# A six-layer cross network on one core: the order of the last but one group's output transposes, and of the first products and sums of the last layer

## The chip, the core and the metric

The kernel runs on one NeuronCore of a Trainium2 chip. It has a matrix engine (PE, with its weight loads shown as PEld), a vector engine (DVE), a scalar engine (ACT), GpSimd (POOL) and a queue engine (SP), which here issues nearly all DMA transfers. Each engine executes its own instructions in order and waits on semaphores for the others. The metric is the device time of one execution in microseconds (us); lower is better. What is compared is the median of several executions.

## The reference

```python
B, F, D, L = 16384, 26, 16, 6          # x0: 16384 x 416, ws: 6 x 416 x 416, bs: 6 x 416, all bfloat16
x = x0
for l in range(L):
    proj = jnp.einsum('bd,de->be', x, ws[l]) + bs[l]
    x = x0 * proj + x
return x
```

Each of the six layers is a 416 x 416 product over 16384 rows, a bias, an elementwise product with `x0` and an elementwise sum with the layer's input.

## The kernel before

The 16384 rows are cut into 8 groups of 2048 (`g` = 0 to 7). Inside the core the data lie transposed: features on the partitions, rows along the free axis. The 416 features are three tiles of 128 (`t` or `i` = 0, 1, 2) and a tail of 32 (`x3`); the four chunks of 512 rows of a group (`j` = 0 to 3) have their tails stacked in one 128-partition tile. A pair (group, layer) is a job; a list written out by hand interleaves the jobs of several groups so that PE always has one that is ready.

A tile of a job is computed by `full` (12 matmuls of 128x128 by 512, line L456) and `rows32` (the tail's 4 matmuls, L477), and read out of PSUM by `evacuate`: ACT adds the bias (L394), DVE multiplies by `x0` (L403) and adds the layer's input (L408). The tails of several jobs are computed together (`tails`, L471, L488, L497; read out by L434, L436, L438).

The program is recorded by `Program.add`: the place where an instruction is recorded is its place in its engine's queue, and its waits follow from the tiles that it reads and writes. Nothing reorders it later, save that DVE's sums in `evacuate` are held back by one product.

**Groups 0 to 6** leave the chip through `output(g)`. The result lies transposed, so SP issues DMA transposes into the tile `ost`: `turn(0)`, `turn(1)` and `turn(2)` (L637), one for each feature tile of 128 x 2048, and one for the tail tile into `ot3` (L643). The tail is then spread over `ost` by a copy (`spread`: POOL for groups 0 to 5, ACT for group 6, L663), and `store` (L672) writes `ost` to HBM. For group 6, the last but one (`g == LAST - 1`), the third tile's transpose comes in two halves, and the spread and the two stores of half a group each are recorded by the caller, after all tiles of layer 4 of group 7. Each of group 6's transposes has a semaphore (lane) of its own.

**Group 7** takes another way in its last layer, so that its result needs no transpose: `nat_full` multiplies with the data as the stationary operand (L797, with the tail and bias matmuls of `nat_rows` at L840 and L845), so rows lie on the partitions. ACT copies each 128 x 416 result out of PSUM (`nat_out`, L851), DVE multiplies two of them by `x0` (`nat_mul`, L857), adds the layer's input (`nat_add`, L863), and `nat_store` (L870) writes four of them out. There are 16 such results: four steps `kk` of four chunks `j`. In step 0 DVE does, for each pair of chunks, the product and then the sum.

The layer's input that `nat_add` needs, `x5n`, must be turned as well, from layer 4's result. Its first two feature tiles are turned by DMA: `rest_turn(0)` and `rest_turn(1)` (L683), issued by SP. Its third tile and its tail are turned on PE (`turn_last`, L808; `turn_tails`, L826) and copied by DVE (L820) and ACT (L818, L833). Every `nat_add` waits for both DMA transposes.

At the end of the program SP's queue holds, in this order:

```
rest_turn(0)      L683   needs tile (7, layer 4, i=0)
turn(0)           L637   needs tile (6, layer 5, i=0)
tail transpose    L643   needs the tail of (6, layer 5)
turn(1)           L637   needs tile (6, layer 5, i=1)
turn(2) in halves L637   needs tile (6, layer 5, i=2)
rest_turn(1)      L683   needs tile (7, layer 4, i=1)
two stores        L672   group 6
four stores       L870   group 7 (a fifth is issued by ACT)
```

The tiles are computed in the order (6, layer 5, i=0), (6, layer 5, i=1), the tails, (6, layer 5, i=2), (7, layer 4, i=1), (7, layer 4, i=2).

Of the kernel before, what the change touches and what calls it, by code (L numbers as in the profile page):

```python
# [21 lines left out]
class Program:  # L22
# [12 lines left out]
    def add(self, eng, fn, reads=(), writes=(), lane=None, batch=None, hold=False, release=False):  # L35
        op = Op(eng, fn, lane, batch)
        deps = {}
        if eng == "pool":
            writes = list(writes) + ["pool"]
        for t in reads:  # L40
            w = self.writer.get(t)
            if w is not None:
                deps[id(w)] = (w, True)
        for t in writes:
            w = self.writer.get(t)
            if w is not None:
                deps[id(w)] = (w, True)
            for r in self.readers.get(t, ()):
                if id(r) not in deps:
                    deps[id(r)] = (r, False)  # L50
        for d, raw in deps.values():
            if d.lane is None and d.eng == eng and lane is None and (eng == "pe" or not raw):
                continue
            op.deps.append(d)
        for t in reads:
            self.readers.setdefault(t, []).append(op)
        for t in writes:
            self.writer[t] = op
            self.readers[t] = []
        if eng == "dve":  # L60
            if hold:
                self.flush()
                self.held = op
            else:
                self.queue[eng].append(op)
                if release:
                    self.flush()
        else:
            self.queue[eng].append(op)
        if lane is not None:  # L70
            batches = self.lanes.setdefault(lane, [])
            if not batches or batches[-1][0] != batch:
                batches.append((batch, []))
            batches[-1][1].append(op)
        return op
# [123 lines left out]
def bass_standalone__cross_network_dcn__recsys_kernel(  # L199
# [14 lines left out]
    LAST = NG - 1  # L214
# [136 lines left out]
    def done_with(g, l):  # L351
        users[(g, l)] = users.get((g, l), 0) + 1
        if users[(g, l)] < 2:
            return
        if l > 0:
            free_x.append(xset[(g, l)])
            free_3.append(xtail[(g, l)])
        prefill(g, l + 1)
        if l == L - 1:
            output(g)  # L360
            if g == 3:
                load_last()
            if 4 < g + NX0 <= LAST:
                load_group(g + NX0)
# [268 lines left out]
    def output(g):  # L633

        s, s3 = xset[(g, L)], xtail[(g, L)]
        def turn(t, j0=0, j1=NJ):
            add("sp", lambda h: h.dma_start_transpose(  # L637
                ost[:, j0 * KK:j1 * KK, t * P:(t + 1) * P], xs[s][:, t * GC + j0 * CH:t * GC + j1 * CH]),
                reads=[("x", s, t, j) for j in range(j0, j1)], writes=[("ost", t, j) for j in range(j0, j1)],
                lane="ot" if g < LAST - 1 else f"ot_{t}{j0}", batch=g)  # L640

        turn(0)
        add("sp", lambda h: h.dma_start_transpose(ot3[:, :, :], x3s[s3][:, :]),  # L643
            reads=[("x3", s3)], writes=["ot3"], lane="ot3", batch=g)
        if g < LAST - 1:
            spread("pool")
        turn(1)
        if g < LAST - 1:
            turn(2)
            store(g, 0, NJ)  # L650
        else:
            turn(2, 0, 2)
            turn(2, 2, NJ)
        free_x.append(s)
        free_3.append(s3)

    def spread(eng):

        dst = ost[:, :, NT * P:D].rearrange("p (j k) f -> p j k f", j=NJ)
        sp_ = ot3[:, :, :].rearrange("p k (j f) -> p j k f", j=NJ)  # L660
        kw = dict(reads=["ot3"], writes=[("ost", NT, j) for j in range(NJ)])
        if eng == "act":
            add("act", lambda h: h.activation(dst, sp_, ACT_F.Copy), **kw)  # L663
        else:
            add(eng, lambda h: h.tensor_copy(dst, sp_), **kw)  # L665

    def store(g, j0, j1):

        rows = out[g * GC + j0 * CH:g * GC + j1 * CH, :]
        o = ost[:, j0 * KK:j1 * KK, :].rearrange("p (j k) f -> p j k f", k=KK)  # L670
        pat = "(j p k) f -> p j k f" if g == 0 else "(j k p) f -> p j k f"
        add("sp", lambda h: h.dma_start(rows.rearrange(pat, j=j1 - j0, k=KK), o),  # L672
            reads=[("ost", t, j) for t in range(NT + 1) for j in range(j0, j1)],
            writes=[("out", g, j0)], lane="out", batch=g)
# [108 lines left out]
    g, l = LAST, L - 1  # L783
# [70 lines left out]
    def nat_mul(kk, j, n=2):  # L854
        o, x0v = on[:, j:j + n, kk, :], x0n7[:, j:j + n, kk, :]
        toks = [("on", a, kk) for a in range(j, j + n)]
        add("dve", lambda h: h.tensor_tensor(o, o, x0v, ALU.mult),  # L857
            reads=toks + [("n7", a) for a in range(j, j + n)], writes=toks)

    def nat_add(kk, j, n=2):  # L860
        o, x5v = on[:, j:j + n, kk, :], x5n[:, j:j + n, kk, :]
        toks = [("on", a, kk) for a in range(j, j + n)]
        add("dve", lambda h: h.tensor_tensor(o, o, x5v, ALU.add),  # L863
            reads=toks + [("x5n", a, t) for a in range(j, j + n) for t in range(NT + 1)], writes=toks)
# [3 lines left out]
    def nat_store(kk, j0, j1, eng="sp"):  # L868
        dst = out[LAST * GC:B, :].rearrange("(j k p) f -> p j k f", j=NJ, k=KK)[:, j0:j1, kk, :]
        add(eng, lambda h: h.dma_start(dst, on[:, j0:j1, kk, :]),  # L870
            reads=[("on", j, kk) for j in range(j0, j1)],
            writes=[("out7", kk, j0)], lane=f"out7_{stores[0]}", batch=0)
        stores[0] += 1
# [18 lines left out]
    turned_out(2, b2)  # L892
    for j in (0, 2):
        nat_mul(0, j)
        nat_add(0, j)
    nat_store(0, 0, NJ)
    nat_rows(1, bks[1])
# [54 lines left out]
```

## Time and profile before

| what | value |
|---|---|
| median of 4 runs | 479.81 us (478.33 to 480.57) |
| the profiled execution | 479.09 us, span 477.3 us |
| granted PE clock | 0.997 |
| PE busy | 468.2 us (98% of the span) |
| DVE busy | 403.7 us (85%) |
| ACT busy | 342.0 us (72%) |
| POOL busy | 6.6 us (1%) |
| PE's share of the chain that ended last | 90% |

The span runs from the first to the last instruction of the profiled execution; its 479.09 us hold 1.8 us more than that. Times below are counted from the span's start. PE is busy almost all the time until 471 us; what follows is the end of group 7: DVE's products and sums, and the stores. Short forms in the views: "SPq" and "ACTq" are the queues in which these engines issue transfers; "idle before <-releaser" gives the time that an engine stood idle before an instruction and what it was waiting for.

### The profile page before, as it was taken

The numbers are of one execution on the slowest core, as the hardware profiler recorded it, in microseconds if no ns is written. First come the engines' busy times: TensorE is split into PE (matmuls) and PEld (weight loads), VectorE is DVE, ScalarE is ACT, GpSimd is POOL, SyncE is SP. The second block draws the span as 40 slices with busy tenths as digits, with TensorE's granted clock in tenths as the row PEclk, the third lists the DMA queues.
The fourth block names the chain that finished last, engine by engine and source line by source line (L and its number), as shares of the span: only waits on it lengthen the run. The fifth ranks groups of instructions, "written<-read, shape, count | busy, mean of one in ns | idle before, by whom it ended". The sixth has DMA issues, their size and how long they took to land.

```text
span 477.3 us, 8393 instructions
## 1 busy us (share of the span) xinstructions
PE 468.2 (98%) x3371; PEld 195.9 (41%) x3371; DVE 403.7 (85%) x696; ACT 342.0 (72%) x372; POOL 6.6 (1%) x15
## 2 busy tenths in 40 slices
PE   7999999999999999999999999999999999999994
PEld 6344444444444444444444444444444444444342
DVE  2888888888888888898889879888888888888877
ACT  3677777777777777777777777777777777777684
POOL 1000000000000000000000000000000000000000
PEclk9999999999999999999999999999999999999998
DMA  8976940630102377379319931980000138026899
GB/s 228 175 161 134 207 86 1 145 77 1 28 7 45 66 215 161 78 151 239 75 26 206 211 89 31 188 246 0 2 15 20 21 64 236 2 45 151 204 143 287
DMA packets 138363, 53.31 MB, mean 112 GB/s; under 512 B 112330, under 2 KB 137428, under 8 KB 138324
## 3 DMA queue, kind: packets, MB, share of 16 engines
q1 hardware_dynamic: 137448, 52.14, 48.8%
q10 hardware_dynamic: 876, 0.64, 0.4%
q8 instruction: 26, 0.43, 0.4%
q14 instruction: 13, 0.11, 0.1%
HBM read 5.97 MB, written 13.63 MB: 41 GB/s over the span
## 4 chain that ended last, share of the span: by engine, by line
PE 90%; SPq 4%; DVE 3%; DMA 2%; ACT 0%; issue 0%; DVEq 0%
PE ps L456 75%; PE ps L477 7%; PE ps L497 7%; SPq L292 2%; DMA x<-x 1%; PE ps L471 1%; DVE x L863 1%; DVE x L857 1%; PE ps L488 1%; SPq L297 1%; DVE tw L403 1%; DVE x L408 1%; SPq L285 1%; SPq L521 0%; ACT tw L394 0%; DMA x<-ost 0%
## 5 line engine op out<-in xcount | busy, mean ns | idle before, releaser
L394 ACT ACTIVATE tw<-ps,bias 128x1024 bf16<-128x1024 f32 (+1 forms) x295 | 299.5, 1070 | 120.2 <-PE ps L477 76.0
L456 PE MATMUL ps<-x,wm 128*128 128x512 bf16 x1692 | 379.4, 380 | 0.4 <-DMA wm<-in_ws_dram 0.4
L456 PEld LDWEIGHTS ps<-x,wm 128*128 128x128 bf16 x1692 | 158.9, 98 | 214.0 <-issue 28.5
L403 DVE TENSOR_TENSOR tw<-tw,x 128x1024 bf16<-128x1024 bf16 (+1 forms) x285 | 192.7, 685 | 53.8 <-ACT tw L394 53.5
L408 DVE TENSOR_TENSOR x<-tw,x 128x1024 bf16<-128x1024 bf16 (+1 forms) x285 | 182.1, 679 | 0.0
L477 PE MATMUL ps<-x,w 32*128 32x512 bf16 x512 | 39.3, 379 | 0.1
L497 PE MATMUL ps<-x,wm 128*32 128x512 bf16 x564 | 33.0, 380 | 0.0
L434 ACT ACTIVATE ts<-ps,bias 128x512 bf16<-128x512 f32 x47 | 28.7, 700 | 0.0
L438 DVE TENSOR_TENSOR x<-ts,x 128x512 bf16<-128x512 bf16 x47 | 18.6, 417 | 3.1 <-DMA x<-x 3.0
L497 PEld LDWEIGHTS ps<-x,wm 128*32 128x32 bf16 x564 | 13.8, 96 | 17.6 <-issue 5.3
L477 PEld LDWEIGHTS ps<-x,w 32*128 32x128 bf16 x512 | 7.8, 92 | 27.7 <-issue 27.1
L436 DVE TENSOR_TENSOR ts<-ts,x 128x512 bf16<-128x512 bf16 x47 | 18.5, 417 | 0.0
L665 POOL COPY ost<-ot 128x512 bf16<-128x512 bf16 x6 | 5.2, 864 | 423.5 <-DMA ot<-x 423.5
L797 PE MATMUL ps<-wm,x 128*128 128x416 bf16 x48 | 9.5, 340 | 0.0
L568 DVE COPY x<-ps 128x512 bf16<-128x512 bf16 x4 | 1.7, 424 | 8.9 <-PE ps L561 8.9
L851 ACT ACTIVATE x<-ps 128x416 bf16<-128x416 f32 x16 | 7.7, 534 | 2.0 <-PE ps L797 1.9
L565 ACT ACTIVATE x<-ps 128x512 bf16<-128x512 bf16 x8 | 4.2, 599 | 5.8 <-PE ps L561 5.8
L863 DVE TENSOR_TENSOR x<-x,x 128x832 bf16<-128x832 bf16 x8 | 4.7, 592 | 2.6 <-DMA x<-x 2.3
L797 PEld LDWEIGHTS ps<-wm,x 128*128 128x128 bf16 x48 | 4.3, 98 | 4.2 <-issue 1.0
L488 PE MATMUL ps<-x,w 32*32 32x512 bf16 x188 | 5.9, 374 | 0.0
L471 PE MATMUL ps<-x,w 32*32 32x512 bf16 x208 | 5.6, 385 | 0.0
L561 PE MATMUL ps<-ident,x 128*128 128x128 bf16 x64 | 5.3, 243 | 0.3 <-ACT x L565 0.3
(38 smaller groups left out, 35.8 us busy)
## 6 DMA issues: line engine op xcount, KB each, us to landing
out_dram<-ost SPq DMA_DIRECT2D x6, 1664.0 KB, 7.0
x<-in_x_dram SPq DMA_DIRECT2D x7, 416.0 KB, 8.0
x<-x SPq DMA_DIRECT2D x24, 96.0 KB, 2.2
out_dram<-ost SPq DMA_DIRECT2D x2, 832.0 KB, 6.6
wm<-in_ws_dram SPq DMA_DIRECT2D x5, 312.0 KB, 3.5
x<-x SPq DMA_DIRECT2D x22, 64.0 KB, 2.0
out_dram<-x SPq DMA_DIRECT2D x3, 416.0 KB, 3.8
x<-ost SPq DMA_DIRECT2D x28, 32.0 KB, 2.3
```

The source lines that it names most:

```text
L394: add("act", lambda h, a=a, w=w, b0=b0: h.activation(tw[r][:, a * CH:(a + w) * CH], psum[:, b0 * CH:(b0 + w) * CH], ACT_F.Identity, bias=b ...
L403: add("dve", lambda h, a=a, e=e: h.tensor_tensor(tw[r][:, a * CH:e * CH], tw[r][:, a * CH:e * CH], x0s[s0][:, i * GC + a * CH:i * GC + e * ...
L408: add("dve", lambda h, a=a, e=e: h.tensor_tensor(xs[so][:, i * GC + a * CH:i * GC + e * CH], tw[r][:, a * CH:e * CH], src(i, a, e), ALU.ad ...
L434: add("act", lambda h: h.activation(ts[r][:, :], bank(b), ACT_F.Identity, bias=bias[:, 3, l:l + 1], scale=1.0), reads=[("ps", b), "bias"], ...
L436: add("dve", lambda h: h.tensor_tensor(ts[r][:, :], ts[r][:, :], x03, ALU.mult), reads=[("ts", r)] + tok0, writes=[("ts", r)], release=True)
L438: add("dve", lambda h: h.tensor_tensor(x3s[so][:, :], ts[r][:, :], res, ALU.add), reads=[("ts", r)] + rtok, writes=[("x3", so), ("x3", so, ...
L456: add("pe", lambda h, t=t, j=j: h.matmul(bank(banks[j]), wm[l][:, t, ecols], src(t, j, j + 1), start=(first and t == 0), stop=(not first a ...
L471: add("pe", lambda h, q=q, j=j, r=r, c=c, o=o: h.matmul(psum[o, banks[j] * CH:(banks[j] + 1) * CH], w3[l][q, i * P + c * T32:i * P + (c + ...
L477: add("pe", lambda h, q=q, j=j, r=r: h.matmul(bank(banks[j]), w3[l][q, ecols], src[q, :], start=first, stop=not first, tile_position=(r * ...
L488: add("pe", lambda h, l=l, b=b, s3=s3, ri=ri, qi=qi, ro=ro, qo=qo: h.matmul(psum[qo, b * CH:(b + 1) * CH], w3[l][qi, NT * P:D], s3[qi, :], ...
L497: add("pe", lambda h, t=t, j=j, src=src, l=l, b=b, ro=ro, qo=qo: h.matmul(psum[qo, b * CH:(b + 1) * CH], wm[l][:, t, NT * P:D], src(t, j, ...
L797: add("pe", lambda h, t=t: h.matmul(bank(b, n=D), xcol(t, j, kk), wm[l][:, t, :], start=(first and t == 0), stop=(not first and t == NT - 1)),
```

## The change

In `output`, for group 6 alone, `turn(1)` is recorded right after `turn(0)`, ahead of the tail's transpose. For the other groups the order stays. In the last layer of group 7, step 0 (four chunks, two to an instruction) does both products before the first sum; in steps 1 to 3 the order stays.

```diff
         turn(0)
+        if g == LAST - 1:
+            turn(1)
         add("sp", lambda h: h.dma_start_transpose(ot3[:, :, :], x3s[s3][:, :]),
             reads=[("x3", s3)], writes=["ot3"], lane="ot3", batch=g)
         if g < LAST - 1:
             spread("pool")
-        turn(1)
-        if g < LAST - 1:
+            turn(1)
             turn(2)
             store(g, 0, NJ)
         else:
@@
     turned_out(2, b2)
     for j in (0, 2):
         nat_mul(0, j)
+    for j in (0, 2):
         nat_add(0, j)
     nat_store(0, 0, NJ)
```

The numbers of instructions on each engine stay the same. Lines from L643 on move by one or two numbers in the changed file (L643 becomes L645, L683 L684, L857 L858, L863 L864).

## The prediction

> **What bounds the kernel now.** The page's list of the chain that ended last comes first: PE has 90% of it, but a change at the very end lives in the other tenth. So I read the chain in order of time over the last 80 us. PE's matmuls run through until 453 us; then the chain leaves PE:
>
> ```profile
> 459.51 0.67 DVE tw L403 x2
> 460.18 0.14 DVE x L408
> 460.32 5.56 DMA x<-x
> 465.88 0.03 issue
> ...
> 466.00 0.59 DVE x L863
> 466.59 0.51 DVE x L857
> ...
> 467.20 0.59 DVE x L863
> ```
>
> The 5.56 us are one transfer, `rest_turn(1)`, from its issue to its landing; DVE's first sum (L863) starts on it, and from there sum and product alternate to the last sum. The timeline of DVE's and ACT's instructions tells how hard that hold is:
>
> ```profile
> 458.22 1.28 DVE L408 TENSOR_TENSOR x<-tw,x 128x1024 bf16<-128x1024 bf16 x2
> 463.09 0.59 DVE L857 TENSOR_TENSOR x<-x,x 128x832 bf16<-128x832 bf16 x1 [0.30 <-ACT x L851]
> 466.00 0.59 DVE L863 TENSOR_TENSOR x<-x,x 128x832 bf16<-128x832 bf16 x1 [2.31 <-DMA x<-x]
> 459.74 0.67 ACT L663 ACTIVATE ost<-ot 128x512 bf16<-128x512 bf16 x1
> 462.13 1.75 ACT L851 ACTIVATE x<-ps 128x416 bf16<-128x416 f32 x4 [0.89 <-PE ps L797]
> 469.56 2.10 ACT L851 ACTIVATE x<-ps 128x416 bf16<-128x416 f32 x4 [0.58 <-PE ps L797]
> ```
>
> DVE sits idle for 2.31 us between its first product and its first sum. ACT has copied out all four results of step 0 by 462.13 + 1.75 = 463.88, and all of step 3 by 471.66, while DVE's last sum starts at 474.10: after the first sum DVE alone sets the pace, with some 2 us of lead on ACT. Third, SP's queue, which issued the transfer:
>
> ```profile
> 449.15 2.94 SPq L637 DMA_TRANSPOSE ost<-x  x1
> 453.92 1.19 SPq L643 DMA_TRANSPOSE ot<-x  x1
> 455.15 5.13 SPq L637 DMA_TRANSPOSE ost<-x  x3
> 460.32 1.94 SPq L683 DMA_TRANSPOSE x<-x  x1
> 462.44 3.23 SPq L672 DMA_DIRECT2D out_dram<-ost  x2
> ```
>
> SP stood still from 452.09 (449.15 + 2.94) to 453.92, waiting for the tail, and then issued without a break. The tile that `rest_turn(1)` turns was ready at 459.50 (458.22 + 1.28), yet it went out at 460.32: 0.8 us behind the queue. Last, the DMA in short stretches (length, granted clock, DMA share, GB/s):
>
> ```profile
> 453.00:455.00 2.00, 1.00 0.02 5
> 456.40:458.70 2.30, 1.00 1.09 209
> 461.50:462.80 1.30, 1.00 1.67 210
> 462.80:464.40 1.60, 1.00 0.94 10
> 464.40:465.30 0.90, 1.00 1.21 273
> ```
>
> From 453 to 455 nothing moved. A whole tile of 524 KB takes some 2.4 us at 209 GB/s. And in the middle of `rest_turn(1)` the transfers all but halt for 1.6 us, from 462.8 to 464.4.
>
> **The change part by part.** No instruction is added or taken away; two are moved.
>
> *`turn(1)` ahead of the tail's transpose (SP).* Its tile is ready when the second L408 of that tile ends, at 452.55 by DVE's timeline; SP is free at 452.09. So it goes out at 452.6. A full transpose that SP issues with nothing behind it has taken 1.39 (455.15) to 1.98 us (446.70), so it is out by 454.0 to 454.6. It holds up one thing, the tail's transpose, ready at 453.88: out 0.1 to 0.7 us later than before, ending at 455.2 to 455.8 with its 1.19 us, or 456.6 with the longest of that line (2.04 us, at 249.97, behind a full one). For whom is that late? The two halves of `turn(2)` wait for DVE's sums at 456.43 and 457.03 anyway, so for them nothing is; and ACT's spread (L663) reads the tail. That copy comes only after ACT's other work, at 459.74. The tail landed 2.4 us after its issue here and 3.5 at most elsewhere, so by 454.6 + 3.5 = 458.1 in the changed order. It costs nothing; without that cover every us after 459.74 would delay ACT by one.
>
> The first half goes out at 456.5, where it went before (456.58): its data hold it. But the halves took 2.02 and 1.62 us to issue because a full tile was still under way ahead of them. With the DMA nearly drained I put a half between the quarter (1.19 us) and the full tile (1.98): 1.45 us each. 456.5 + 2 x 1.45 = 459.4, just ahead of `rest_turn(1)`'s data at 459.50. So `rest_turn(1)` goes out at 459.55, 0.77 us earlier. The bounds: 0.1 us if the halves take their old 2.02 + 1.62 us (456.5 + 3.64 = 460.2), and 0.8 us at best, by the data.
>
> *What the landing makes of it.* In the profile the first packets came 1.2 us after the issue (460.32 to 461.5). From 459.55 they start at 460.7. By 462.8 they have run 2.1 us x 209 GB/s = 439 of 524 KB. If the halt stays where it is, the remaining 85 KB go after 464.4 at 273 GB/s, in 0.3 us: 464.7, and 0.5 us to the landing (465.4, where by the packets' sizes the stores take over, to 465.88) give 465.2 instead of 465.88. So 0.7 us. Does the halt stay? In the packets of 462.3 to 462.7 there is one of 16 KB on an instruction queue (q8). The same kind of packet stands at 300.1 and 265.4, with transposes under way, and there too the DMA fell to 6 GB/s (301.2 to 302.2) and 9 GB/s (266.3 to 267.0). It follows a place in an engine's program, and PE's program and times are not touched, so I keep the halt at 462.8 to 464.4. Bounds: nothing gained, if the halt pins the landing; and, if the transfer passes whole, 460.7 + 2.4 + 0.5 = 463.6, 2.3 us earlier.
>
> The Trainium skill ("DMA: Bandwidth & Descriptors", section "Queues, rings and completion order") says that a DMA engine takes turns between its queues packet by packet. By that rule a fetch on another queue costs the transpose one turn of one engine and no halt; the sum would then be that of the case below in which the transfer clears the halt, 477.8 us. The 10 GB/s over 1.6 us speak against it, and the rows decide.
>
> *Both products ahead of the first sum (DVE).* The second product (chunks 2 and 3) needs ACT's fourth copy, done at 463.88; it then runs at 463.9 to 464.5, inside DVE's idle 2.31 us. Queued behind its wait are the first sum and all after it, so no sum can start before 464.5; the landing at 465.2 is later, and the wait costs nothing. Were the landing before 464.5, the rest would be lost. What is saved is one product behind the landing. First sum to the third product took 467.71 - 466.00 = 1.71 us; with two sums in a row at 0.51 to 0.59 us each it takes about 1.1. That is 0.6 us; bounds 0.5 (one 0.51 us step) and 0.7 (the step and the pauses at 467.1).
>
> *The sum.* 0.7 + 0.6 = 1.3 us of the chain. Does it reach the end? The final product needs ACT's last copy at 471.66; it would then start at 473.78 - 1.3 = 472.5, so ACT stays ahead. The stores: the DMA is full with stores from 465.4 on, at 329 to 360 GB/s, but had a gap (122 GB/s) from 472.8 to 473.4. All stores stand behind `rest_turn(1)` in SP's queue and start 0.7 us earlier with it; the last but two would then follow without the gap, the final one, from ACT, still starts when its sum is done. So the 1.3 us hold: 479.09 - 1.3 = 477.8 for the execution profiled (span 476.0). That execution lies 0.7 us under the median of its four, so against the median I say 479.81 - 1.3 = 478.5 us.
>
> **The rivals.** *The landing doesn't move* (0.15): SP issues the halves as slowly as before, or the halt decides when the transfer ends. For it: 1.6 of the 5.56 us are halt, which no order of issue touches. Against: what is left behind the halt shrinks with every packet sent ahead of it. Only the products are left: 479.81 - 0.6 = 479.2.
>
> *The transfer clears the halt* (0.23): if the instruction fetch comes a little later, or the packets run at 273 instead of 209 GB/s, it all lands by 463.6. Then the second product binds: first sum at 464.55 instead of 466.00, 1.45 + 0.6 = 2.05 us. ACT gives the same ceiling: last copy 471.66, product and sum 0.36 + 0.04 + 0.59, end 472.7 instead of 474.69. 479.81 - 2.0 = 477.8.
>
> *Slower: ACT waits for the tail* (0.07). The tail's transpose now stands behind a full tile, and ACT's spread stands ahead of the copies of the last layer (L833, L851). If it lands at Y, ACT is late by Y - 459.74, and so are its last copy and DVE's end; with the 2.0 us of lead it is a loss from Y = 461.7 on. The longest landing of any transpose in the trace is 9.8 us (L292): 454.6 + 9.8 = 464.4, ACT 4.7 us late, a loss of 2.7 us, 482.5. Against it: this line's landings of 2.4 to 3.5 us. The change not doing what it says can be left out: SP's and DVE's queues hold it.
>
> **How the numbers follow.** The forecast has 0.47, the three cases 0.15, 0.23 and 0.07; 0.08 is left for what I don't see. A measurement of this kernel can tell about 0.5%, 2.4 us, from no change; the four runs before lie 2.2 us apart. No case of mine reaches 2.4 us by itself, so faster by more than that needs some of that scatter: a fifth of the forecast (0.10), under half of the case with 2.0 us (0.10), 0.04 of the rest: 0.24. Slower by more: most of the slower case and a part of the unseen, 0.08. Within: 0.68. The range goes from 476.8 (the ceiling of 2.0 us and 1 us of scatter) to 480.0 (products alone and 0.8 us of scatter).
>
> **What would show it.** Right: `turn(1)` issued near 452.6, DMA busy from 453.8; `rest_turn(1)` issued near 459.55; one L857 at 463.9 in the idle time; two sums in a row after a landing near 465.2; last sum ending near 473.4. Wrong: `rest_turn(1)` at 460.2 or later (halves still slow); a landing at 465.9 in spite of an early issue; the halt gone; or ACT's L663 starting after 459.74 with idle time ahead of it, which would turn the gain round.

## The result and the profile after

| | before | changed |
|---|---|---|
| median | 478.89 us (79 runs, 477.94 to 481.66) | 478.06 us (48 runs, 476.82 to 480.95) |
| ratio | | 0.9982 (95% interval 0.9975 to 0.9990) |
| profiled execution, span | 479.09 us, 477.3 us | 478.27 us, 476.5 us |
| first `rest_turn` issued | 446.70 | 446.82 |
| `rest_turn(1)` issued, landed | 460.32, 465.88 | 459.66, 465.76 |
| last sum ends | 474.69 | 473.87 |

The change makes the kernel faster by 0.18%, 0.86 us: clear of the comparison's uncertainty, and less than the 1.3 us that the prediction added up. The changed kernel's work up to the end ran 0.12 us later in its profile, so below I count from the issue of the first `rest_turn`, just ahead of the part that changed. Counted so, the last sum came 0.95 us earlier (28.00 to 27.05 us) and the end of the program 0.94 us.

SP's queue in the changed kernel:

```profile
449.28 5.62 SPq L637 DMA_TRANSPOSE ost<-x  x2
454.95 1.56 SPq L645 DMA_TRANSPOSE ot<-x  x1
456.59 2.66 SPq L637 DMA_TRANSPOSE ost<-x  x2
459.66 1.81 SPq L684 DMA_TRANSPOSE x<-x  x1
461.66 1.79 SPq L673 DMA_DIRECT2D out_dram<-ost  x2
```

`turn(1)` goes out in what was SP's idle time, the two halves of `turn(2)` take 2.66 us to issue, not 3.69 as before, and `rest_turn(1)` leaves right when its tile is done: 12.84 us after the first `rest_turn`, where it was 13.62. The DMA in short stretches (length, granted clock, DMA share, GB/s) shows the filled gap, and no halt during the transfer of `rest_turn(1)`:

```profile
453.00:455.00 2.00, 1.00 0.64 120
460.80:463.20 2.40, 1.00 1.06 199
463.20:463.70 0.50, 1.00 1.17 248
463.80:465.80 2.00, 1.00 1.08 325
472.00:473.00 1.00, 1.00 0.62 204
```

From 463.8 on the DMA is already full of stores. Yet the chain of waits still holds the transfer until 465.76:

```profile
459.64 0.03 DVE tw L403
459.66 6.09 DMA x<-x
465.76 0.03 issue
...
465.88 0.06 DVE x L864
465.94 0.45 issue
466.39 0.59 DVE x L864
466.97 0.51 DVE x L858
```

6.09 us from issue to landing, where it was 5.56. DVE's timeline shows the rest of the change at work:

```profile
463.22 0.59 DVE L858 TENSOR_TENSOR x<-x,x 128x832 bf16<-128x832 bf16 x1 [0.30 <-ACT x L852]
464.04 0.59 DVE L858 TENSOR_TENSOR x<-x,x 128x832 bf16<-128x832 bf16 x1 [0.23 <-ACT x L852]
465.88 1.09 DVE L864 TENSOR_TENSOR x<-x,x 128x832 bf16<-128x832 bf16 x2 [1.25 <-DMA x<-x]
466.89 0.58 DVE L858 TENSOR_TENSOR x<-x,x 128x832 bf16<-128x832 bf16 x1
```

The second product runs inside the wait, and from the first sum to the third product it is 1.01 us instead of 1.71. DVE still waits 1.25 us for the transfer after its second product.

Why does a transfer whose bytes have nearly all moved by 463.7 land at 465.76? A DMA runs on 16 engines, and each reports its part. The trace has these reports, and the packets that the engines moved around them:

```
reports of rest_turn(1), changed kernel: 464.06 to 464.16 (15 of them), 465.76 (the last)
last 256-byte packet of the transposes:  463.72
instruction fetch, 16384 bytes:          463.73, took 0.95 us
last 4-byte packets (reports) behind it: 464.66, 464.67
reports of rest_turn(1), before:         465.77 to 465.88 (all 16); fetch at 462.42, took 1.25 us
```

The trace names no engine for a packet, but the times follow on each other: it seems that one engine took up a fetch of 16 KB, just after its last piece of the transpose and ahead of its report, and the landing is that of the last of 16. The other 15 were done 1.6 us earlier. The fetch itself is 0.95 us of that; what the rest is the trace does not show. Before, the fetch at the same place of the program came in the middle of the transfer, and the whole transfer halted for 1.6 us. It is taken for a fetch of PE: its queue has 26 such packets for PE's 6760 recorded instructions, and the records between two of them number 256 on the mean. The experiments below, which add and remove PE instructions, move it.

So the theory that I took to the experiments: the fetch costs `rest_turn(1)` some 1.6 us in either order of issue, so that the moved transposes give next to nothing, and the products nearly all.

### The profile page after: what moved, and what is told of

Its sections match the earlier page's. It is cut to its first block, busy times and chain, and to the rows that moved or that the text cites. A ratio compares the mean times of both kernels' runs of the same rounds, so it can differ in the third digit from the quotient of the medians.

```text
span 476.5 us, 8393 instructions
## 1 busy us (share of the span) xinstructions
PE 468.8 (98%) x3371; PEld 196.0 (41%) x3371; DVE 403.7 (85%) x696; ACT 342.0 (72%) x372; POOL 6.8 (1%) x15
## 4 chain that ended last, share of the span: by engine, by line
PE 94%; DVE 2%; DMA 1%; ACT 1%; issue 0%; POOL 0%; POOLq 0%; DVEq 0%
PE ps L456 77%; PE ps L477 7%; PE ps L497 7%; DMA x<-x 1%; PE ps L471 1%; DVE x L864 1%; PE ps L561 1%; DVE x L858 1%; PE ps L488 1%; PE ps L541 1%; DVE x L408 1%; ACT tw L394 0%; DVE tw L403 0%; ACT x L565 0%; POOL ident L510 0%
## 5 line engine op out<-in xcount | busy, mean ns | idle before, releaser
L864 DVE TENSOR_TENSOR x<-x,x 128x832 bf16<-128x832 bf16 x8 | 4.6, 591 | 1.4 <-DMA x<-x 1.2
```

## The experiments

### One part of the change at a time

`turn_only` has the first hunk of the diff alone, `products_only` the second.

> The transposes' order of the change alone; step 0 keeps product, sum, product, sum. Fetch theory (the landing of rest_turn(1) is set by one DMA engine that a 16 KB instruction fetch of PE holds up for about 1.6 us, in either order of issue): rest_turn(1) is issued near 459.6, about 0.7 us earlier than before, but lands no more than 0.3 us earlier, and the time is the one before to within 0.3 us (ratio 0.9993 to 1.0). Forecast's theory (the landing follows the issue): landing near 465.2, the time 0.7 us less, ratio 0.9985.

> The order of products and sums of the change alone; SP's queue as before. Fetch theory: the landing stays at 465.9, one product is done in the idle time, first sum to third product 1.0 us instead of 1.7, the time 0.7 us less, ratio 0.9985: nearly all that the whole change gives. Rival (the gain of the whole change needs both parts, since the stores at the end can only follow earlier if the queue does): less than 0.3 us, ratio above 0.9993.

Measured in one comparison (before: 478.68 us; here and below the ratios with their 95% intervals are those of the comparison, not quotients of the medians beside them): `turn_only` 479.13 us, ratio 1.0009 (0.9995 to 1.0022); `products_only` 478.27 us, ratio 0.9986 (0.9975 to 0.9998). DVE in `turn_only`:

```profile
463.03 0.59 DVE L858 TENSOR_TENSOR x<-x,x 128x832 bf16<-128x832 bf16 x1 [0.30 <-ACT x L852]
465.63 0.59 DVE L864 TENSOR_TENSOR x<-x,x 128x832 bf16<-128x832 bf16 x1 [2.01 <-DMA x<-x]
466.14 0.58 DVE L858 TENSOR_TENSOR x<-x,x 128x832 bf16<-128x832 bf16 x1
```

and in `products_only`:

```profile
464.03 0.59 DVE L857 TENSOR_TENSOR x<-x,x 128x832 bf16<-128x832 bf16 x1 [0.23 <-ACT x L851]
465.61 1.09 DVE L863 TENSOR_TENSOR x<-x,x 128x832 bf16<-128x832 bf16 x2 [0.99 <-DMA x<-x]
466.62 0.58 DVE L857 TENSOR_TENSOR x<-x,x 128x832 bf16<-128x832 bf16 x1
```

With the transposes alone the transfer goes out at 459.47 and takes 6.03 us: landing 0.3 us earlier than before by the common count, as the fetch theory had it, and no gain that can be measured. The form was another, though: no single part came late, all 16 reports came at 465.37 to 465.51, and the DMA nearly stood still just after the fetch (463.43, 0.96 us):

```profile
463.40:464.40 1.00, 1.00 1.10 336
464.50:465.30 0.80, 1.00 1.48 55
```

With the products alone the interval holds the whole change's ratio; it reaches to 0.9998, so that the rival of under 0.3 us is excluded only by the profile, in which the end came 0.82 us earlier. Its landing wasn't at 465.9, as expected, but at 465.49, 5.05 us after the issue: in this execution the fetch came at 461.89 and held up the half transpose ahead of it (5.0 us to its landing, before 3.7). The forecast's theory of 0.7 us from the transposes has fallen; that the fetch is the reason is not shown yet.

### Moving the fetch, first way: more PE instructions at the start

```diff
-    keep_busy(14, 7)
...
+    def pad(n):
+        for _ in range(n):
+            add("pe", lambda h: h.matmul(
+                psum_t(7)[:, 0:T32], ident[0:T32, :], ident[0:T32, 0:T32], is_transpose=True,
+                tile_position=(0, 0)),
+                reads=["ident"], writes=[("ps", 7)])
+    pad(81)
+    keep_busy(6, 7)
```

on the kernel before (`before_fetch_moved`) and on the changed one (`after_fetch_moved`). The results that PE writes there are used by nobody.

> The kernel before with 146 more PE instructions at the start (81 transposes of 32x32 added, 8 of the 14 warm-up matmuls left out), so that PE's fetches fall 146 instructions earlier in its program: one near 452, one after 465, none during rest_turn(1). Fetch theory: rest_turn(1), issued near 460.3 on the same clock, lands 4.0 to 4.5 us later instead of 5.6, no 1.6 us halt, and the last sum ends 1.2 to 1.5 us earlier, counted from PE's last product of layer 4; the total less what the start loses. Rival (the halt belongs to the transposes or to the stores behind them in the queue): landing still 5.5 to 6 us after the issue.

> The changed kernel with the same 146 more PE instructions at the start. Fetch theory: rest_turn(1) lands about 4.4 us after its issue instead of 6.1, the first sum starts right after the second product, 1.2 us earlier than in the changed kernel, and against the kernel before with the same instructions added it gains 0.9 to 1.4 us: the order of the transposes then pays. Rival: landing still near 6 us after the issue, and the same 0.8 us of gain as without the added instructions.

Measured (before: 478.68 us): 479.82 us, ratio 1.0019 (1.0008 to 1.0029), and 479.30 us, 1.0011 (1.0002 to 1.0021): the start loses 0.8 and 1.3 us (the first `rest_turn` goes out at 447.54 and 448.14). The fetches came at 451.76 and 452.36, and the next at 470.09 and 470.25. `rest_turn(1)` landed 4.74 and 4.39 us after its issue; in `before_fetch_moved` that was a little more than the 4.0 to 4.5 us expected, and its last sum came 0.80 us earlier, not 1.2 to 1.5. In `after_fetch_moved` DVE no longer waits for the landing. The transfer in the chain of waits of `before_fetch_moved`:

```profile
461.17 4.74 DMA x<-x
```

and DVE in `after_fetch_moved`:

```profile
465.35 0.59 DVE L867 TENSOR_TENSOR x<-x,x 128x832 bf16<-128x832 bf16 x1 [0.23 <-ACT x L861]
465.86 1.09 DVE L873 TENSOR_TENSOR x<-x,x 128x832 bf16<-128x832 bf16 x2
467.09 0.59 DVE L867 TENSOR_TENSOR x<-x,x 128x832 bf16<-128x832 bf16 x1
```

The first sum follows the second product at once. The rival, that the long landing belongs to the transposes or to the stores behind them, has fallen. The gain that was expected of the changed order with the fetch away (0.9 to 1.4 us) was met in the last sum (27.20 against 26.14 us after the first `rest_turn`: 1.06 us), and not at the end of the program (30.32 against 29.53: 0.79 us) nor in the medians (0.5 us). So something else held the end.

### Moving the fetch, second way: fewer PE instructions on the way

In the tiles that stand just ahead of a batch of tails the tail's rows are multiplied in 16 small matmuls; in the first five of these tiles 4 wide ones now do the same.

```diff
+    wide = [n for n in sorted(mode) if mode[n] == "F1"][:5]
...
-            rows32(g, l, i, banks, False, mode[n] == "F1")
+            rows32(g, l, i, banks, False, mode[n] == "F1" and n not in wide)
```

`after_halves` has, on the changed kernel, `rest_turn(1)` in two halves of two chunks, each with its own semaphore; `after_halves_fetch_later` has both.

```diff
+        for j0, j1 in ([(0, NJ)] if t == 0 else [(0, 2), (2, NJ)]):
...
-                writes=[("x5n", j, t) for j in range(NJ)], lane=f"x5_{t}", batch=0)
+                writes=[("x5n", j, t) for j in range(j0, j1)], lane=f"x5_{t}{j0}", batch=0)
```

> The changed kernel with 120 PE instructions fewer: in the first five tiles ahead of a batch of tails the tail's rows are multiplied in 4 wide matmuls instead of 16 small ones. PE's fetches then come 120 instructions later in its program, the last one near 470 us instead of 463. Fetch theory: rest_turn(1) lands about 4.4 us after its issue instead of 6.1, the first sum follows the second product without a wait, 1.2 us earlier than in the changed kernel; 0.5 us or more of that reaches the end (the stores are then nearly without gaps), ratio to the kernel before 0.996 to 0.9975 if the five tiles cost nothing. Rival (fetches don't matter, the earlier landing seen with added instructions came from the shift of the start): landing near 6 us after the issue, ratio 0.998 as for the change.

> The kernel before with the same 120 PE instructions fewer. Fetch theory: rest_turn(1) lands about 4.6 us after its issue instead of 5.6, the time falls by 0.8 to 1.0 us, ratio near 0.998, without any change of order. Rival: as the kernel before, ratio 1.0, landing 5.5 us or more after the issue.

> The changed kernel with rest_turn(1) in two halves of two chunks each, each with its own semaphore. The first half needs only the first half of its tile and of the wait: it lands near 463 us, ahead of the fetch, and the first sum runs near 464.7 instead of 465.9; the second sum still waits for the second half, near 465.5. Fetch theory: a gain of some 0.3 to 0.6 us over the changed kernel, ratio 0.997 to 0.9975. Rival (the landing is not what holds the end any more): same as the changed kernel, 0.998.

> Both: halves and the 120 PE instructions fewer. Neither landing holds DVE any more: first sum right after the second product, near 464.6. Then ACT's last copy near 471.7 and the stores set the end; no better than with the later fetch alone by more than 0.3 us; ratio 0.995 to 0.997. If the stores bind, DMA's share stays at 1.0 or above from 465 to 474 and the last store lands more than 2.3 us after the last sum.

Measured in one comparison (before: 478.68 us): `after_fetch_later` 478.50 us, ratio 0.9995 (0.9986 to 1.0004); `before_fetch_later` 478.96 us, 1.0014 (0.9997 to 1.0031); `after_halves` 477.74 us, 0.9990 (0.9978 to 1.0002); `after_halves_fetch_later` 478.79 us, 1.0009 (0.9992 to 1.0025).

The landings came as the fetch theory says (4.47 and 4.43 us after the issue), the times did not. In `after_halves` the fetch (462.13) came before the first half had landed, and that half landed at 463.96, not near 463 as expected. A fetch hit another transfer too: in the eight profiles of this document with one at 451.75 to 452.50, `turn(0)` landed 5.79 to 6.55 us after its issue, in the six others 4.44 to 4.50. DVE's sums do not wait for that one.

Two things are seen. In the changed kernel with the halves or with the fetch away, the last sum always ends 26.13 or 26.14 us after the first `rest_turn`: here ACT's copies set the pace. DVE's last products in `after_fetch_later` show it:

```profile
470.14 0.59 DVE L865 TENSOR_TENSOR x<-x,x 128x832 bf16<-128x832 bf16 x1
470.65 0.79 DVE L859 TENSOR_TENSOR x<-x,x 128x416 bf16<-128x416 bf16 x2
...
471.99 0.65 DVE L859 TENSOR_TENSOR x<-x,x 128x416 bf16<-128x416 bf16 x2
```

The first pair of step 3 takes 0.79 us, not 0.65, since its second product waits for ACT's second copy (ACT's four run from 469.99 to 472.09, so it ends near 471.04). And the end of the program stays at 29.5 to 29.7 us all the same; the stretch from the last sum to the end grows from 2.6 to 3.4 us and more. In `after_fetch_later` the late fetch shows why. It came at 469.29, in the middle of the stores, and 15 of the 16 parts of the last store landed by 475.38, the last at 476.22. In `after_halves`, with the fetch at 462.13, the parts of the stores land nearly together, but the DMA has no gap left from 464.3 to 474.4.

### Is it the laggard, or the stores' bandwidth?

The laggard theory says that a fetch sets one DMA engine back, and that this engine stays behind to the end while the queue is full of stores. Its rival is that all 16 engines together move the stores as fast as they can. With six tiles instead of five (`[:6]`), and then with eight (`[:8]`), I tried to move the fetch out of the stores as well.

> The changed kernel with 144 PE instructions fewer (six tiles with wide matmuls for the tail's rows instead of five), so that PE's last two fetches come 24 instructions later than with five: one near 453.5, between two transposes, and the one at 469 to 470 falls past PE's last instruction. Laggard theory (the 16 KB fetch holds up one DMA engine by about 1 us wherever the DMA is full, in the transposes or in the stores): all 16 parts of the last store land together, the last sum ends 26.1 us after the first rest_turn's issue as with five tiles, and the program ends 28.7 to 28.9 us after it instead of 29.6; ratio to the kernel before 0.9955 to 0.997, about 0.9 us better than the changed kernel. Rival (the stores' bandwidth alone is the floor): 29.5 us after it, as all variants with an early landing had; ratio 0.998 to 0.9995.

> The kernel before with the same 144 PE instructions fewer. Laggard theory: landing 4.4 to 4.6 us after the issue, last sum 26.9 us and end 29.4 to 29.6 us after the first rest_turn's issue (kernel before: 28.0 and 30.6), ratio near 0.998: a gain of the size of the change without any change of order. Rival: end 30.2 us after it, as with five tiles, ratio 1.0 or above.

> The changed kernel with rest_turn(1) in halves and 144 PE instructions fewer. The transfers have no gap left from 464 to 474 and ACT's last copy sets the last sum at 26.1 us after the first rest_turn's issue, so the halves add nothing to after_fetch_gap: end 28.7 to 29.0 us after it in both, ratios within 0.0005 of each other. If the halves win by more, the landing was still holding something.

> The changed kernel with 192 PE instructions fewer (eight tiles with wide matmuls for the tail's rows). With six tiles the fetches stayed near 452.5 and 469.7; 48 more instructions should bring the first to 455 to 457, between turn(1) and turn(2), and the last past PE's last instruction. Laggard theory: rest_turn(1) lands 4.4 to 4.8 us after its issue, the 16 parts of each of the last stores land within 0.5 us of each other (1.2 us apart with a fetch at 469.7), and the program ends 28.7 to 29.2 us after the first rest_turn's issue, 0.5 to 0.9 us less than the changed kernel. Rival (bandwidth of the stores alone): 29.5 to 29.9 us even with no fetch after 457. If a fetch still falls near 469, the run tells nothing of this.

With six tiles this missed: the fetches came at 452.50 and 469.65, 452.08 and 469.77, 452.09 and 470.18, nearly where they were with five. Measured (before: 478.95 us) 478.61 us, ratio 0.9988 (0.9971 to 1.0005), 479.56 us, 1.0015 (0.9995 to 1.0035), and 478.99 us, 1.0006 (0.9987 to 1.0024); ends at 29.88, 30.27 and 29.89 us. These three tell the two theories apart no better than the ones before; they repeat that the landing (4.46 and 4.45 us for the whole transfer) and ACT's ceiling hold.

With eight tiles it came out: the fetch at 457.53, and none after it. Measured (before: 478.79 us) 478.28 us, ratio 0.9991 (0.9979 to 1.0003). The DMA from the stores' beginning, in `after_no_late_fetch`:

```profile
466.50:468.50 2.00, 1.00 1.08 341
468.50:470.50 2.00, 1.00 1.10 333
470.50:472.50 2.00, 1.00 1.11 332
472.50:474.50 2.00, 1.00 1.11 330
474.50:476.70 2.20, 0.98 0.31 106
```

and in `after_fetch_later`, with a fetch at 469.29:

```profile
466.50:468.50 2.00, 1.00 1.09 332
468.50:470.50 2.00, 1.00 1.11 326
470.50:472.50 2.00, 1.00 0.96 297
472.50:474.50 2.00, 0.90 0.71 231
474.50:476.70 2.20, 0.50 0.19 64
```

Without the fetch all 16 engines are busy at 330 to 341 GB/s until 474.5, and the parts of the last store land between 475.90 and 476.23. With it the rate falls to 297 and 231 GB/s while one engine is still behind. The end comes 28.88 us after the first `rest_turn`, 0.76 us earlier than in the changed kernel and 0.7 earlier than in `after_fetch_later`, with the last sum at the same 26.14. So in these two profiles the laggard theory holds, and the floor of 29.5 us was not bandwidth alone. Nor is the laggard all of it: `after_halves` has no fetch among the stores either, and ended at 29.49. There the fetch had nearly stopped the DMA just ahead of the stores (20 GB/s from 462.4 to 463.6), and behind that the stores ran at 336 GB/s to 474.4; that this lost time is what its end is late by is likely, and not shown. The time of `after_no_late_fetch` gains nothing from its earlier end, because the eight tiles cost about as much on the way: the first `rest_turn` goes out at 447.84, 1.0 us later.

All runs by the common count:

| kernel | PE's fetch | `rest_turn(1)`: issue to landing | last sum | end |
|---|---|---|---|---|
| before | 462.42 | 5.56 | 28.00 | 30.58 |
| changed | 463.73 | 6.09 | 27.05 | 29.64 |
| `turn_only` | 463.43 | 6.03 | 27.69 | 30.28 |
| `products_only` | 461.89 | 5.05 | 26.80 | 29.76 |
| `before_fetch_moved` | 451.76, 470.09 | 4.74 | 27.20 | 30.32 |
| `after_fetch_moved` | 452.36, 470.25 | 4.39 | 26.14 | 29.53 |
| `before_fetch_later` | 451.75, 469.67 | 4.43 | 26.87 | 30.24 |
| `after_fetch_later` | 452.04, 469.29 | 4.47 | 26.14 | 29.58 |
| `after_halves` | 462.13 | 4.80, 4.31 (halves) | 26.13 | 29.49 |
| `after_halves_fetch_later` | 452.33, 469.71 | 3.33, 3.27 (halves) | 26.14 | 29.71 |
| `before_fetch_gap` | 452.08, 469.77 | 4.45 | 26.86 | 30.27 |
| `after_fetch_gap` | 452.50, 469.65 | 4.46 | 26.14 | 29.88 |
| `halves_fetch_gap` | 452.09, 470.18 | 3.38, 3.39 (halves) | 26.14 | 29.89 |
| `after_no_late_fetch` | 457.53 | 4.45 | 26.14 | 28.88 |

(The fetches at the trace's own times, the last two columns in us after the issue of the first `rest_turn`. Times of the whole kernel also hold what the edits cost ahead of that point.)

No version beat the changed kernel beyond the uncertainty: `after_halves` has the lowest median, 477.74 us, but its interval, 0.9978 to 1.0002, takes in the changed kernel's 0.9982.

## Why the prediction was right where it was, and wrong where it was not

**The issue of `rest_turn(1)`: right.** 0.77 us earlier was said, 0.78 us it was by the common count. The halves of `turn(2)` took 1.28 and 1.34 us to issue (said 1.45), and the tile's data, not the queue, released the transfer.

**The forecast's figure: in part luck.** The forecast was 478.5 us and 478.06 was measured, although the gain was 0.86 us and not 1.3. The 1.3 us were taken off the 479.81 us of four runs; the 79 runs beside the changed kernel have a median of 478.89, from which the same sum would have said 477.6.

**The landing: the step that failed.** The prediction had the halt stay at 462.8 to 464.4, with only the last 85 KB behind it, and so 0.7 us of gain. Measured: 0.25 us by the common count (19.18 to 18.93 us). Even that is not shown to be the work of the order: in `products_only`, with the old order, the landing was at 18.68 us, so two executions of one order differ by 0.5 us.

No halt came in the middle; the fetch came 1.2 us later by the common count, behind the last packet of the transposes, and one of 16 reports came late. Both a landing near 465.9 in spite of an early issue and the halt gone were on the prediction's own list of signs of being wrong. The reasoning that PE's program and times are not touched, so that the halt stays where it is, was the weak point: in the five profiles with PE's program unchanged the fetch came 15.08 to 16.91 us after the first `rest_turn` (15.72 and 15.08 with the old order of transposes, 16.91 and 16.80 with the new, 15.69 with the new one and halves). What sets this was not tried. (A small slip beside it: 524 KB at 209 GB/s are 2.5 us, not 2.4.) The row was read rightly as a fetch, and the experiments with the fetch elsewhere show it: in seven profiles without a fetch during it, the whole transfer landed 4.39 to 4.74 us after its issue; in four with one during it, just ahead of it or just behind its last packet, 5.05 to 6.09.

The page of the Trainium skill that the prediction weighed ("DMA: Bandwidth & Descriptors", section "Queues, rings and completion order") says that an engine takes turns between its queues, and in its section "Why a DMA increments its semaphore by 16 and not by 1" that each engine reports its own part. The changed kernel's trace agrees with both: the DMA went on at 325 GB/s from 463.8 on, and one part of 16 came 1.6 us late. The halt of all engines in the kernel before, 10 GB/s for 1.6 us, is not in that rule, nor is the one in `turn_only`.

**The products: right, slightly larger.** 0.6 us was said with 0.7 as the upper bound; 0.70 us it was (1.71 to 1.01 us). The second product ran at 464.04, within the wait, as said.

**The sum.** 0.25 + 0.70 = 0.95 us, which is what the last sum and the end gained in these two executions; the comparison's 0.86 us agrees. The forecast was 1.3 us, so the moved transposes, alone 1.0009 (0.9995 to 1.0022), account for the miss. The rival that the landing does not move and the products alone are left, with 0.6 us and a chance of 0.15, came nearest in the gain.

**The other rivals.** The slower case did not come: ACT's spread began at 459.87 without idle time ahead of it, since the tail's transpose landed at 457.75, ahead of the 458.1 allowed for. It went out 0.9 us later by the common count, not 0.1 to 0.7, as `turn(1)` took 2.20 us to issue, not 1.98 at most.

```profile
455.44 4.58 ACT L394 ACTIVATE tw<-ps,bias 128x512 bf16<-128x512 f32 x7 [0.21 <-PE ps L456]
459.87 0.67 ACT L664 ACTIVATE ost<-ot 128x512 bf16<-128x512 bf16 x1
```

These are ACT's rows in the changed kernel: no wait is shown ahead of the spread. In the changed kernel the condition of the case in which the transfer clears the halt came about: the fetch was later, and all packets had passed by 463.72. Yet 15 of 16 reports came at 464.06 to 464.16, not by 463.6, and the last held the landing to 465.76. Where the experiments let it land early, the case was right about ACT's ceiling: ACT's copies did hold the last sum (26.13 or 26.14 in every such run of the changed order, 1.9 us less than before, said 2.0). What it missed were the stores: the end gained only 0.7 to 1.1 us of it, and 1.7 us in `after_no_late_fetch` alone. The claim that "the 1.3 us hold" through the stores held for the 0.95 us that came (0.94 at the end); for 1.3 it is doubtful, since in `products_only` the last sum gained 1.20 us and the end 0.82.

**Left open.** Why the same fetch halts all 16 engines in one execution and delays only one in another was not tried. Nor was a way to move the fetch that costs nothing ahead of it.

## What to carry to other kernels

A transfer that the end waits for lands with the slowest of its 16 parts: before its earlier issue is booked as a gain, look for what else one DMA engine will be asked for meanwhile, instruction fetches included. What is moved into an idle wait of the engine that sets the end (here one product of 0.59 us) is the safer half of such a change. And a gain ahead of the last stores is worth only what these can follow: count the stretch from the last sum to the end too.

## What was not expected of the hardware

A 16 KB instruction fetch took 0.9 to 1.8 us in these traces, and costs the transfer under way there 0.3 to 1.7 us of landing (5.05 to 6.09 against 4.39 to 4.74 us). With the queue full of stores some of the parts stay behind to the end: the 16 parts of the last store landed over 0.7 to 1.3 us with a fetch at 469 to 470, over 0.2 to 0.5 us with none after 464. The number of PE instructions ahead of it thus moved the end by 0.7 us (29.58 to 28.88 us after the first `rest_turn`, one profile of each) with the same work from there on.
